# Logit matmuls of the last segment as sixteen 32 by 32 tiles in place of four 32 by 128 tiles

## The chip, the cores and the metric

The kernel runs on one core of one Trainium2 chip. The metric is the time of one execution in device microseconds. A core has a matrix engine (TensorE; PE in the profile, with its weight loads in a row of their own, PEld), VectorE (DVE), ScalarE (ACT), GpSimd (POOL) and a queue for transfers (SP). A matmul multiplies a stationary operand, brought in by a weight load, with a moving operand, of which it takes one column after the other. The array may be used whole or as smaller tiles; the profile writes the rows and columns in use as 128*32 or 32*128.

## The reference

The input is x, 2048 tokens of 512 features, in bfloat16. Two branches are computed from it and mixed by a gate per token.

```python
q, k, v = x @ wq, x @ wk, x @ wv           # 32 heads of 16 features, 4 segments of 512 tokens
for s in range(4):                         # branch a: attention within a segment, and a memory
    logits = einsum('bhqd,bhkd->bhqk', qs, ks) * 16 ** -0.5 + mask
    a_dot = softmax(logits) @ vs
    a_mem = (phi(qs) @ M) / (phi(qs) @ z + 1e-6)
    o[s] = sigmoid(beta) * a_mem + (1 - sigmoid(beta)) * a_dot
    M += phi(ks).T @ vs ; z += phi(ks).sum()
a = o @ wo
b = (gelu(x @ w_gate) * (x @ w_up)) @ w_down        # branch b: 512 -> 1792 -> 512
out = g * a + (1 - g) * b                  # g = sigmoid of a weighted sum of x per token
```

The mask is causal. phi(t) is t + 1 for positive t and exp(t) otherwise.

## The kernel before

All engines follow one written order of tasks (`ORDER`): each word is a task with its engine and its buffers, and the tasks of an engine run in that order. On TensorE the tasks of attention and of the feed-forward branch alternate: groups of q, k, v, gate (`gt`) and up projections (`up`), logit slots (`lg0` to `lg71`), the products with the probabilities (`pv`), memory updates (`M`), memory reads (`den`, `num`), and the down projection with the output projection (`dn`, `wo`). Nearly all of them use four tiles of 128 rows by 32 columns side by side: the helper `mm4` (L385) splits one 128 by 128 matmul into four with 32 output partitions each. The first matmuls of the kernel, up to the first logit slot, use the whole array.

Queries and keys lie transposed in chunks of 128 partitions: 8 heads of 16 features, 512 tokens. A group of 32 partitions holds an even and an odd head. For even heads the stationary operand is 16 rows of `kT`; for odd heads it is 32 rows of `kO`, a copy of the keys with the even head's rows set to zero.

A segment has 18 logit slots, 9 for each pair of chunks. In a slot (`logit_slot`) the loop over `j` goes over the four groups of 32 partitions, thus four heads, and each of the four writes to a PSUM bank of its own (two `lg` tiles of two banks). Only the parts of the triangle that the mask leaves are computed. The slots are of two kinds:

- whole-key slots (`e` is 0 for even heads and 1 for odd heads): 128 keys by 256, 192 or 64 queries. A slot has three parts of these widths in one of two orders, `FULL[0]` (256, 64, 192) or `FULL[1]` (256, 192, 64). That makes 3 x 4 = 12 matmuls with 16 or 32 rows and 128 columns, and 512 moving columns for each `j`. There are 16 of these in a segment.
- merged slots (`e` is 2), two in a segment: 8 parts of 64 queries, 32 matmuls.

After a slot ACT takes the exponential of its two `lg` tiles (L233), POOL sets what the mask forbids to zero (L715, L710), and `pv` uses the result as moving operand (L743). The slots of the last segment are `lg54` to `lg71`, of which `lg56` and `lg65` are merged ones. They begin at 193.3 us and end at 240 us of the span; behind them TensorE has memory reads, products with probabilities and down projections up to 265 us.

The matmuls of a memory update (L858) have 34 moving columns: 8 quads of four column tiles, 32 matmuls in a group.

Of the kernel before, what the change touches and what calls it, by code (L numbers as in the profile page):

```python
# [13 lines left out]
P = 128  # L14
# [5 lines left out]
NSEG = 4  # L20
# [141 lines left out]
class Sched:  # L162
# [10 lines left out]
    def add(self, name, engs, fn, **kw):  # L173
        t = Task(name, [engs] if isinstance(engs, str) else list(engs), fn, **kw)
        self.tasks.append(t)
        return t
# [22 lines left out]
def kernel(  # L199
# [15 lines left out]
    nc = tc.nc  # L215
# [10 lines left out]
    def act(dst, src, func, **kw):  # L226


        k = 1 if func == AF.Gelu_apprx_tanh else 0
        if k != aset[0]:  # L230
            nc.scalar.activation(nil[0][:, 1:2], nil[0][:, 0:1], func)  # L231
            aset[0] = k
        nc.scalar.activation(dst, src, func, **kw)  # L233
# [21 lines left out]
    def lgtile(name="lg"):  # L255
        return plg.tile([P, 2, L], F32, name=name, tag="lg" + S.bank())
# [4 lines left out]
    def rtile(ring, shape, dtype=BF):  # L261
        return rp.tile(shape, dtype, name=ring, tag=ring + S.bank(), bufs=1)
# [398 lines left out]
    def logit_slot(s, t):  # L661
        pr, u = divmod(t, 9)
        gi = s * NSLOT + t
        A = LGT[(s, t)] = {}
        e, w = {0: (0, 0), 1: (0, 1), 3: (1, 0), 4: (1, 1), 5: (0, 0), 6: (0, 1), 7: (1, 0),
                8: (1, 1), 2: (2, 0)}[u]
        cs = [0, 1] if e == 2 else [0 if u < 5 else 1]

        def fn(_):
            TAB["tiled"] = True  # L670
            for h in range(2):
                A[h] = lgtile()
            q, k, o = (QK.get((n, s, pr)) for n in "qko")
            if e == 2:
                parts = [(i, kt, kt * P, HB, (4 * i + kt) * HB) for i in cs for kt in range(KT)]
            else:
                parts = [(cs[0], kt, kt * P + HB + d, n, at) for kt, d, n, at in FULL[w]]
            for i, kt, q0, n, at in parts:
                for j in range(4):
                    a = slice(32 * j, 32 * j + (DH if e == 0 else 32))  # L680
                    l = (k[a, i, kt * P:(kt + 1) * P] if e == 0 else
                         o[a, i, kt, 0:P] if e == 2 else o[a, i, kt, HB:HB + P])
                    nc.tensor.matmul(A[j // 2][:, j % 2, at:at + n], lhsT=l,  # L683
                                     rhs=q[a, i, q0:q0 + n],
                                     start=True, stop=True, tile_position=(32 * j, 0))
        deps = []
        for i in cs:
            c = 2 * pr + i
            deps += [EVQK[(n, s, c)] for n in ("qk", "qo", "qeo")[e]]
        frees = []  # L690
        if gi > 0:
            deps.append(LT[gi - 1])
        if u == 8:
            frees = [(n + "T" if n != "o" else "kO", first_ev[(n, s, pr)]) for n in "qko"]
            if s == 0:
                frees = [((r, pr) if r == "kT" else r, x) for r, x in frees]
        g = add(f"lg{gi}", "PE", fn, cost=240, deps=deps, mode="row",
                alloc=["lg", "lg"], frees=frees)
        LT[gi] = g
        for h in range(2):  # L700
            def fx(_, h=h):
                pT[(s, t, h)] = rtile("pT", [P, 2, L])
                act(pT[(s, t, h)][:, :, :], A[h][:, :, :], AF.Exp, scale=0.25)

            def fa(_, h=h):
                pt = pT[(s, t, h)]
                if e == 2:
                    for z in range(2):
                        v = pt[HB * z:HB * z + HB, :, :].rearrange("p h (g n) -> p (h g) n", n=HB)
                        nc.gpsimd.affine_select(out=v, in_=v, pattern=[[0, 16], [1, HB]],  # L710
                                                compare_op=ALU.is_ge, fill=0.0, base=0,
                                                channel_multiplier=-1)
                    return
                v = pt[:, :, :].rearrange("p h (g n) -> p (h g) n", g=2)[:, :, 0:HB]
                nc.gpsimd.affine_select(out=v, in_=v, pattern=[[0, 4], [1, HB]],  # L715
                                        compare_op=ALU.is_ge, fill=0.0, base=HB,
                                        channel_multiplier=-1)
            x = add(f"ex{gi}{'ab'[h]}", "ACT", fx, kind="exp",
                    deps=[g], alloc=["pT"], frees=[(("lg", h), g)])
            XT_[(gi, h)] = x  # L720
            AT[(gi, h)] = add(f"as{gi}{'ab'[h]}", "POOL", fa,
                              kind="as8" if e == 2 else "as2", deps=[x])
# [371 lines left out]
```

## Time and profile before

| | |
|---|---|
| median of 3 runs | 270.33 us (270.03 to 270.43) |
| the profiled execution | 270.36 us, span 268.6 us |
| granted TensorE clock | 1.000 |
| PE matmuls | 6,276, busy 262.6 us (98% of the span) |
| PE weight loads | 6,276, busy 143.5 us |
| DVE, ACT, POOL busy | 182.7, 222.0, 142.7 us |
| logit matmuls (L683) | 1,024 in 72 slots |
| of these in the slots that the change touches | 192 in 16 slots |

The profile is one execution. A matmul's duration in it runs from its beginning to the modelled end of its results, so matmuls that run side by side or behind each other overlap, and the busy share of PE is not its share of peak. How fast matmuls follow one another is read from their beginnings. Every matmul has its weight load just ahead of it in program order; "pair" below means the two. "Quad" is four matmuls of four tiles that begin within some ns of each other.

### The profile page before, as it was taken

The numbers are of one execution on the slowest core, as the hardware profiler recorded it, in microseconds if no ns is written. First come the engines' busy times: TensorE is split into PE (matmuls) and PEld (weight loads), VectorE is DVE, ScalarE is ACT, GpSimd is POOL, SyncE is SP. The second block draws the span as 40 slices with busy tenths as digits, with TensorE's granted clock in tenths as the row PEclk, the third lists the DMA queues.
The fourth block names the chain that finished last, engine by engine and source line by source line (L and its number), as shares of the span: only waits on it lengthen the run. The fifth ranks groups of instructions, "written<-read, shape, count | busy, mean of one in ns | idle before, by whom it ended". The sixth has DMA issues, their size and how long they took to land.

```text
span 268.6 us, 13714 instructions
## 1 busy us (share of the span) xinstructions
PE 262.6 (98%) x6276; PEld 143.5 (53%) x6276; DVE 182.7 (68%) x367; ACT 222.0 (83%) x260; POOL 142.7 (53%) x262
## 2 busy tenths in 40 slices
PE   8999999999999999989999999999999999999994
PEld 7645455454565545464554546555554555545653
DVE  1552799967776688867876949765785896284712
ACT  2699999999989999999998999987989897882010
POOL 8440665047589166578427275557517287954100
PEclk9999999999999999999999999999999999999999
DMA  6999949322300000200004000200100000100111
GB/s 208 370 242 307 171 45 159 101 83 43 120 2 5 2 2 2 45 2 5 2 4 44 22 2 19 68 5 2 43 5 2 2 2 5 61 4 8 58 51 52
DMA packets 23610, 15.96 MB, mean 59 GB/s; under 512 B 13824, under 2 KB 22528, under 8 KB 23552
## 3 DMA queue, kind: packets, MB, share of 16 engines
q1 hardware_dynamic: 22400, 14.17, 22.7%
q8 instruction: 49, 0.80, 1.3%
q10 hardware_dynamic: 1152, 0.92, 1.0%
q14 instruction: 9, 0.07, 0.1%
HBM read 9.84 MB, written 2.10 MB: 44 GB/s over the span
## 4 chain that ended last, share of the span: by engine, by line
PE 88%; ACT 5%; DVE 4%; issue 1%
PE dn L385 23%; PE up L385 18%; PE gt L385 14%; PE lg L683 8%; PE pv L743 7%; PE v L385 5%; PE q L385 4%; PE k L385 4%; PE k L381 2%; ACT pT L233 2%; ACT L231 1%; ACT G L233 1%; PE num L385 1%; PE warm L381 1%; DVE ebr L622 1%; DVE G L610 1%
## 5 line engine op out<-in xcount | busy, mean ns | idle before, releaser
L233 ACT ACTIVATE pT<-lg 128x1024 bf16<-128x1024 f32 x144 | 137.7, 1029 | 11.1 <-PE lg L683 7.4
L715 POOL TENSOR_SCALAR_AFFINE_SELECT pT<-pT 128x256 bf16<-128x256 bf16 x128 | 52.5, 436 | 61.9 <-ACT pT L233 60.3
L385 PE MATMUL dn<-wdn,G 128*32 128x512 bf16 (+1 forms) x952 | 57.0, 367 | 0.0
L385 PE MATMUL up<-xT,wup 128*32 128x512 bf16 x896 | 56.6, 380 | 0.0
L610 DVE TENSOR_TENSOR G<-up,G 128x512 bf16<-128x512 f32 x56 | 38.5, 687 | 19.8 <-PE up L385 19.0
L385 PE MATMUL gt<-xT,wga 128*32 128x512 bf16 x832 | 48.0, 379 | 0.1
L710 POOL TENSOR_SCALAR_AFFINE_SELECT pT<-pT 64x1024 bf16<-64x1024 bf16 x32 | 37.1, 1160 | 16.5 <-ACT pT L233 11.0
L760 DVE STREAM_TRANSPOSE T<-pv 128x512 f32<-128x512 f32 x32 | 22.7, 711 | 17.8 <-PE pv L743 17.7
L385 PEld LDWEIGHTS <-wga 128*32 128x32 bf16 x832 | 23.4, 97 | 20.7 <-issue 0.4
L385 PEld LDWEIGHTS <-G 128*32 128x32 bf16 x952 | 23.9, 97 | 19.4
L385 PEld LDWEIGHTS <-wup 128*32 128x32 bf16 x896 | 22.9, 96 | 19.4 <-issue 0.2
L233 ACT ACTIVATE G<-gt 128x1024 bf16<-128x1024 f32 x28 | 27.5, 1016 | 3.4 <-PE gt L385 3.3
L231 ACT ACT_TABLE_LOAD x20 | 25.7, 1283 | 0.4
L743 PE MATMUL pv<-pT,vz 128*32 128x256 bf16 (+2 forms) x768 | 22.5, 238 | 0.1
L998 ACT ACTIVATE osb<-dn,omz 128x512 bf16<-128x512 f32 (+1 forms) x6 | 3.7, 616 | 20.8 <-PE dn L385 20.8
L743 PEld LDWEIGHTS <-vz 128*32 128x32 bf16 x768 | 17.2, 97 | 5.8 <-issue 0.6
L385 PEld LDWEIGHTS <-xT 128*32 128x32 bf16 x528 | 13.4, 96 | 12.2 <-DVE xT L786 0.2
L385 PE MATMUL dn<-wo,xT 128*32 128x512 bf16 (+1 forms) x272 | 19.1, 367 | 0.0
L923 POOL TENSOR_SCALAR rm<-Tm 32x32 f32<-32x32 f32 x48 | 15.1, 315 | 7.3 <-DVE Tm L917 4.2
L683 PEld LDWEIGHTS <-kO 32*128 32x128 bf16 x640 | 9.7, 92 | 15.7 <-issue 14.9
L743 PE MATMUL pv<-pT,vh 128*32 128x64 bf16 x512 | 17.6, 193 | 0.0
L683 PE MATMUL lg<-qT,kO 32*128 32x64 bf16 (+2 forms) x640 | 16.9, 217 | 0.5 <-issue 0.5
(107 smaller groups left out, 335.7 us busy)
## 6 DMA issues: line engine op xcount, KB each, us to landing
wup<-in_B_w_up_dram SPq DMA_DIRECT2D x1, 1792.0 KB, 9.4
out_dram<-osb SPq DMA_DIRECT2D x13, 128.0 KB, 1.8
wdn<-in_B_w_down_dram SPq DMA_DIRECT2D x3, 512.0 KB, 4.0
wga<-in_B_w_gate_dram SPq DMA_DIRECT2D x1, 1280.0 KB, 9.5
wdn<-in_A_x_dram SPq DMA_DIRECT2D x2, 512.0 KB, 10.9
wq<-in_A_wq_dram SPq DMA_DIRECT2D x1, 512.0 KB, 4.5
wga<-in_B_w_gate_dram SPq DMA_DIRECT2D x1, 512.0 KB, 5.8
wv<-in_A_wv_dram SPq DMA_DIRECT2D x1, 512.0 KB, 6.7
```

What stands on the lines that cost most here:

```text
L231: nc.scalar.activation(nil[0][:, 1:2], nil[0][:, 0:1], func)
L233: nc.scalar.activation(dst, src, func, **kw)
L381: nc.tensor.matmul(out, lhsT=lhsT, rhs=rhs, start=start, stop=stop)
L385: nc.tensor.matmul(out[a], lhsT=lhsT[:, a], rhs=rhs, start=start, stop=stop, tile_position=(0, 32 * j), skip_group_check=True)
L610: UPT[(s, hs)] = evac("DVE", g, box, lambda e, t: nc.vector.tensor_mul(G[(s, hs // 2)][:, hs % 2, :], t[:, :], G[(s, hs // 2)][:, hs % 2, ...
L683: nc.tensor.matmul(A[j // 2][:, j % 2, at:at + n], lhsT=l, rhs=q[a, i, q0:q0 + n], start=True, stop=True, tile_position=(32 * j, 0))
L710: nc.gpsimd.affine_select(out=v, in_=v, pattern=[[0, 16], [1, HB]], compare_op=ALU.is_ge, fill=0.0, base=0, channel_multiplier=-1)
L715: nc.gpsimd.affine_select(out=v, in_=v, pattern=[[0, 4], [1, HB]], compare_op=ALU.is_ge, fill=0.0, base=HB, channel_multiplier=-1)
L743: nc.tensor.matmul(t[32 * j:32 * j + 32, q0:q0 + n], lhsT=v, rhs=pT[(s, u, j // 2)][:, j % 2, at:at + n], start=(n_ == 0), stop=(n_ == len ...
L760: nc.vector.transpose(TT[key][:, e, :, :].rearrange("p a b -> p (a b)"), t[:, :])
L923: eng_of[e].tensor_scalar_add(RMt[s][32 * j:32 * j + 32, c, :, :], bx["Td"][32 * c:32 * c + 32, :, 2 * j:2 * j + 2], 1e-6)
L998: nc.scalar.activation(bx["o"][:, lo:hi], box["t"][:, 0:hi - lo], AF.Copy, scale=g)
```

## The change

In the last segment's whole-key slots each matmul of 32 (or 16) rows by 128 columns is split into four by columns: the loop over `b` takes 32 keys at a time as stationary operand and writes their 32 output partitions, with the same moving operand. So a part of a slot has 16 matmuls, on tiles of 32 by 32 of the array, in place of 4. All other slots run the loop once, as before.

```diff
-                    nc.tensor.matmul(A[j // 2][:, j % 2, at:at + n], lhsT=l,
-                                     rhs=q[a, i, q0:q0 + n],
-                                     start=True, stop=True, tile_position=(32 * j, 0))
+                    for b in range(4) if s == NSEG - 1 and e < 2 else [None]:
+                        m = slice(0, P) if b is None else slice(32 * b, 32 * b + 32)
+                        nc.tensor.matmul(A[j // 2][m, j % 2, at:at + n], lhsT=l[:, m],
+                                         rhs=q[a, i, q0:q0 + n], start=True, stop=True,
+                                         tile_position=(32 * j, 32 * b if b else 0),
+                                         skip_group_check=b is not None)
```

The matmuls of the 16 slots go from 192 to 768, and the weight loads with them. The tasks, their order and their buffers are the same.

## The prediction

> **What bounds the kernel now.** I read the page's engine table first, then the chain that ended last, cut to the last segment, then the timeline of single slots.
>
> ```profile
> span 268.6 us, 13714 instructions
> PE 262.6 (98%) x6276; PEld 143.5 (53%) x6276; DVE 182.7 (68%) x367; ACT 222.0 (83%) x260; POOL 142.7 (53%) x262
> PE 88%; ACT 5%; DVE 4%; issue 1%
> PE dn L385 23%; PE up L385 18%; PE gt L385 14%; PE lg L683 8%; PE pv L743 7%; PE v L385 5%; PE q L385 4%; PE k L385 4%; PE k L381 2%; ACT pT L233 2%; ACT L231 1%; ACT G L233 1%; PE num L385 1%; PE warm L381 1%; DVE ebr L622 1%; DVE G L610 1%
> ```
>
> TensorE (PE) is busy all the time and carries 88% of the chain. Cut to 190 us and after, the chain is PE without a break up to 265.1 us, where the last evictions and stores follow. The table of waits from 185 us on has no entry for PE, and its weight loads wait for another engine twice, 0.6 us together. So what a logit slot of the last segment costs or saves on PE moves the end one for one: behind the last slot PE still has 25 us of work queued, mostly down projection. Here is that chain around three slots (start, length, what, instructions):
>
> ```profile
> 222.50 0.22 PE up L385 x4
> 222.72 0.33 PE lg L683 x12
> 223.05 0.76 PE dn L385 x12
> 223.81 0.86 PE up L385 x16
> 224.67 0.36 PE lg L683 x32
> 225.03 0.98 PE dn L385 x16
> ```
>
> A slot of 12 matmuls costs 0.33 us, and the merged slot of 32 matmuls of 64 columns (which the edit leaves alone) only 0.36. The timeline of one slot with what stands on both sides of it (PE only; a row's length runs to the end of its last matmul, which includes the pipeline's depth):
>
> ```profile
> 206.07 0.39 PE L385 MATMUL v<-wv,xT 128*32 128x512 bf16 x4
> 206.39 0.40 PE L683 MATMUL lg<-qT,kO 32*128 32x256 bf16 x12
> 206.72 1.05 PE L385 MATMUL up<-xT,wup 128*32 128x512 bf16 x16
> ```
>
> A quad of 512 columns elsewhere begins 0.215 us after the one before (0.86 us for 16 `up` matmuls above), so 0.42 ns per column: 107, 80 and 27 ns for 256, 192 and 64. The slot's first matmul begins 0.31 us after the last `v` quad, not 0.215: about 0.10 us of standstill on the way in. Its last matmul has 64 columns and takes 188 ns by the grouped rows, so it begins 0.40 - 0.19 = 0.21 after the first; with its 27 ns that is 0.24, and the next group begins at 0.33: 0.09 standstill on the way out. In between, 512 columns cost 215 ns plus some 11 ns for the first exposed weight load. In the 16 slots of the segment these lengths repeat to a few ns; slots that end with 192 columns also take 0.33.
>
> **What the change does to this.** In 16 slots (18 of the segment less the two merged ones; 8 run 256, 64, 192 columns, 8 run 256, 192, 64) each of the 3 parts gets 16 pairs of weight load and matmul in place of 4. A slot goes from 12 to 48 pairs, PE from 12,552 instructions to 13,704 (+576 of each kind). Nothing moves: order, banks, waits and the other engines' instructions are as before. The columns streamed per tile stay 512 per slot, so the data time stays 215 ns if 16 tiles run beside each other as 4 do now. Three terms are left.
>
> *Standstill in and out.* Both sides of the slot are 128x32 tiles, the slot becomes 32x32: columns agree, rows still don't. Does the row change alone cost the 0.10? The trace has one such case, the first slot, entered from full 128x128 matmuls (only the rows change):
>
> ```profile
> 14.32 0.38 PE L381 MATMUL q<-xT,wq 128*128 128x512 bf16 x1
> 14.63 0.40 PE L683 MATMUL lg<-qT,kT 16*128 16x256 bf16 x12
> 14.96 0.61 PE L385 MATMUL v<-wv,xT 128*32 128x512 bf16 x7
> ```
>
> Again 0.31 from the last 512 columns to the slot. I take both standstills as unchanged: 0. The way out by a row change alone is not in the trace; bounds 0 and -0.09 us per slot.
>
> *Issue of the pairs.* This is the term that decides. How fast can PE take pairs of load and matmul when the columns are few? The update matmuls `M` (34 columns, 32 pairs, four column tiles) show two paces. One that begins right behind a logit slot:
>
> ```profile
> 175.23 0.38 PE L858 MATMUL M<-vz,pk 128*32 128x34 bf16 x32
> ```
>
> 0.38 less 0.18 for the last matmul: 32 pairs begin in 0.20 us, 6.3 ns each. But behind another `M` group at 44.57 the loads of the gate stream come slower. The weight loads in windows that end at 44.80 and at 44.842:
>
> ```profile
> 44.79 0.09 PEld L385 LDWEIGHTS <-wga 128*32 128x32 bf16 x1
> 44.79 0.13 PEld L385 LDWEIGHTS <-wga 128*32 128x32 bf16 x6
> ```
>
> Five more loads in 0.13 - 0.09 = 0.04 us, with the matmuls between them: the single records stand 8.3 ns apart per pair, 4.1 ns per instruction, and this goes on until 512-column quads let the stream catch up. I read it as a short queue that PE's sequencer fills at 8.3 ns per pair. In the group at 175.23 the sequencer delivers 0.20 / 8.3 = 24 pairs, so about 8 of the 32 lay ready when the standstill ended. For a changed slot: 8 pairs ready, 40 x 8.3 = 332 ns until the last pair begins. The data doesn't hold this up: part two could begin at 120 ns, and its first pair is fed at 75; from its seventh pair on the feed is later than the tile. Then the last tile streams 80 or 27 ns and the 0.09 follows: 0.332 + 0.172 = 0.504 and 0.332 + 0.118 = 0.450, against 0.330. That is +0.174 and +0.120, times 8 each: **+1.39 + 0.96 = +2.35 us**. A matmul behind a just-issued load may add its 8 to 10 ns once (the `up` quad behind a slot is that much late): +0.1 in all. I take +2.4.
>
> Bounds: if the queue were deep enough for the whole slot, the pairs would follow at the 3.6 ns at which the four of a quad begin. Then 256, 64, 192 has its last tile at 120 + 58 + 56 = 234 ns (158 now) and 256, 192, 64 at 120 + 82 + 56 = 258 (212 now): +0.076 and +0.046, **+1.0 us** in 16 slots. If only 8 tiles run at once, each part streams twice: +215 ns and some 60 of skew, 16 x 0.275 = **+4.4 us**. I stay with the feed, the only pace seen past the ready pairs.
>
> *Fetching.* The page has 0.80 MB of instruction packets, 64 bytes for each of PE's 12,552; 1,152 more are 0.07 MB, some 5 packets of 49, and the DMA engines are busy for 0.05 of the stretch from 185 to 242 us: 0. Uncovered, one packet's wait would be a few tenths of a us.
>
> What waits for the slots: the exponentials on ACT start up to 0.17 us later, and so does everything behind them on PE itself, so no new wait; the probabilities are used by PE some slots later.
>
> **Sum.** The profiled execution took 270.36 us (span 268.6 and 1.8 around it), 0.03 above the median of 270.33. 270.36 + 2.4 = 272.8 us, and the difference to the median doesn't matter. A run of this kernel can tell about 0.2%, 0.54 us, from no change.
>
> **Rivals.**
> *The pairs aren't fed, but free* (271.4 us, +1.0, worked out above). For: the queue's depth is inferred from one group; the merged slot begins 32 pairs in 0.23 us with no sign of lack. Against: 32 pairs at 7 ns barely outrun the feed, and 48 do. The Trainium skill, "TensorE: Matmul & The Clock Gate", "Measured speedup vs the span model", counts about 4 ns per further tile and sixteen tiles at 10.6 times one; by that rule alone this rival is the result. The row at 44.79 speaks for a slower pace, and no run here yet shows sixteen tiles. Chance 0.13.
> *Only four tiles of the sixteen run at once.* All traffic of the trace has four in flight: four row tiles or four column tiles. If tiles that share rows queue behind each other, each part streams four times: +3 x 215 = +645 ns a slot, 16 x 0.65 = +10.4, 280.8 us. Against: the four column tiles of `up` share all 128 rows and run side by side. The Trainium skill, same page, "The mechanism", says that a weight load overlaps a running matmul only when its row group differs, which would bring this about; the `up` rows contradict it for the loads of column tiles. Chance 0.09; eight at once (274.8) 0.05.
> *Faster: no standstill.* If the array halts only when the tiles' columns change, 32x32 between 128x32 needs neither the 0.10 nor the 0.09. Per slot 0.147 - 0.188 = -0.04, in sum -0.66: 269.7 us. It decides from 0.15 us saved per slot up. Against it stands the entry at 14.63. Chance 0.05. With the way out alone saved, +0.9: 271.3, inside the range.
> The change does what it says: the listing of after has the 1,152 instructions in these slots and no other.
>
> **How the numbers follow.** Fed pairs 0.68 (272.8, own range 271.9 to 273.6), free pairs 0.13, eight 0.05, four 0.09, no standstill 0.05. The range 271.2 to 275.0 takes in the first three, and leaves out four at once and no standstill. Faster by over 0.2%: 0.03, the larger part of the last case; its rest and small surprises in the cost, 0.03 for the same; slower 0.94.
>
> **What would show it.** After: 16 logit slots of 48 pairs at 0.50 and 0.45 us on the chain in place of 0.33, entry still 0.31 behind the last quad; loads and matmuls 8 ns apart past the first eight pairs; the merged slots still 0.36; all other groups the same. Slots of 0.40 mean a deeper queue, of about 1 us serial tiles, under 0.33 that the standstill has gone.

## The result and the profile after

The changed kernel takes 276.44 us (median of 4 runs, 275.03 to 276.88) against 270.25: ratio 1.022, 95% interval 1.0201 to 1.0240. A second set of five runs, with a second trace, gave 277.19 us, ratio 1.025 (1.0232 to 1.0267). The forecast was 272.8 with a range up to 275.0: the direction was right, and the loss is between two and three times the forecast one.

The profiled execution took 276.88 us. From its page, the lines of the span, of PE, of the instruction packets and of the chain:

```profile
span 275.2 us, 14866 instructions
PE 267.4 (97%) x6852; PEld 149.3 (54%) x6852; DVE 182.2 (66%) x367; ACT 222.7 (81%) x260; POOL 141.1 (51%) x262
q8 instruction: 53, 0.87, 1.3%
PE 80%; SPq 6%; DMA 6%; DVE 4%; ACT 3%; issue 1%; ACTq 0%
```

PE has 576 matmuls and 576 weight loads more, as the diff says, and 53 instruction packets in place of 49. In the segment the chain is still PE's; the transfers in it belong to the start of the kernel. The slot `lg58`, the same one that the prediction showed, with its neighbours (timeline, PE only):

```profile
207.96 0.60 PE L385 MATMUL v<-wv,xT 128*32 128x512 bf16 x8
208.49 0.62 PE L685 MATMUL lg<-qT,kO 32*32 32x256 bf16 x48
209.05 0.40 PE L385 MATMUL up<-xT,wup 128*32 128x512 bf16 x4
```

The next group begins 0.56 us after the slot, not 0.33. The single records of the slot: it begins 309 ns after the last `v` quad (311 before), its last matmul begins 429 ns after its first (213 before), and the `up` quad 125 ns later (117 before). So the way in is what it was, the way out is 8 ns longer, and the inside has doubled. Cut into narrow windows, the timeline shows how. The first row ends its window at 208.665, the second one at 208.78:

```profile
208.49 0.41 PE L685 MATMUL lg<-qT,kO 32*32 32x256 bf16 x32
208.49 0.41 PE L685 MATMUL lg<-qT,kO 32*32 32x256 bf16 x32
```

32 matmuls have begun by 208.665, and none begins in the following 0.115 us. In the single records the first 16 begin within 50 ns, 3.3 ns apart; the second 16 from 119 to 169 ns; then no load and no matmul begins until 304 ns (the 33rd weight load had begun at 143), and from there the pairs follow 8.3 ns apart. The sixteen tiles run beside each other as hoped; the stop in the middle is new.

There is a second new thing. The chain a little later:

```profile
223.04 0.56 PE pv L746 x40
223.59 0.24 PE lg L685 x11
223.84 0.79 issue
224.63 0.36 PE lg L685 x30
```

For 0.79 us PE waits for nothing that the profile shows ("issue"). A like stop lies in a `pv` group at 216.83, 0.61 us long by the single records.

From the beginning of `lg54` to the last matmul the kernel before takes 71.45 us, the changed one 76.79 in this trace and 78.39 in the second. The split slots make up 8 x (0.609 - 0.330) + 8 x (0.555 - 0.330) = 4.0 of the 5.3 and 6.9; the rest, 1.3 and 2.9, is as much as the stops for "issue" amount to beyond the time that would have passed anyway. The first trace had also lost 1.3 us before the segment began (`lg54` at 194.61 against 193.33), where both kernels are the same; in the second trace it begins at 193.36, so that part is the run's.

### The profile page after: what moved, and what is told of

It reads as the page before. It is cut to its first block, busy times and chain, and to the rows that moved or that the text cites. A ratio compares the mean times of both kernels' runs of the same rounds, so it can differ in the third digit from the quotient of the medians.

```text
span 275.2 us, 14866 instructions
## 1 busy us (share of the span) xinstructions
PE 267.4 (97%) x6852; PEld 149.3 (54%) x6852; DVE 182.2 (66%) x367; ACT 222.7 (81%) x260; POOL 141.1 (51%) x262
## 4 chain that ended last, share of the span: by engine, by line
PE 80%; SPq 6%; DMA 6%; DVE 4%; ACT 3%; issue 1%; ACTq 0%
PE dn L385 22%; PE up L385 17%; PE gt L385 12%; PE lg L685 9%; PE pv L746 7%; DMA beta<-in_A_beta_dram 4%; SPq L295 4%; PE v L385 4%; PE q L385 4%; PE k L385 4%; DMA wdn<-in_A_x_dram 2%; ACT pT L233 2%; SPq L323 1%; PE num L385 1%; DVE ebr L622 1%
## 5 line engine op out<-in xcount | busy, mean ns | idle before, releaser
L718 POOL TENSOR_SCALAR_AFFINE_SELECT pT<-pT 128x256 bf16<-128x256 bf16 x128 | 51.0, 423 | 68.7 <-ACT pT L233 67.2
L385 PEld LDWEIGHTS <-wga 128*32 128x32 bf16 x832 | 24.8, 97 | 19.0 <-DMA wga<-in_B_w_gate_dram 0.2
L385 PEld LDWEIGHTS <-xT 128*32 128x32 bf16 x528 | 13.7, 96 | 12.3 <-issue 0.7
L685 PEld LDWEIGHTS <-kO 32*128 32x128 bf16 (+1 forms) x928 | 11.6, 91 | 16.3 <-issue 14.9
L685 PE MATMUL lg<-qT,kO 32*128 32x64 bf16 (+5 forms) x928 | 19.0, 224 | 0.5 <-ACT pT L233 0.4
```

The source lines that it names most:

```text
L385: nc.tensor.matmul(out[a], lhsT=lhsT[:, a], rhs=rhs, start=start, stop=stop, tile_position=(0, 32 * j), skip_group_check=True)
L685: nc.tensor.matmul(A[j // 2][m, j % 2, at:at + n], lhsT=l[:, m], rhs=q[a, i, q0:q0 + n], start=True, stop=True, tile_position=(32 * j, 32 ...
```

## The experiments

Three theories. **1**: PE holds at most 64 instructions (32 pairs) that have not finished; the 33rd pair gets in when the first matmul ends. (Here every matmul has one load, so no run can tell a limit of 64 instructions from one of 32 matmuls.) **2**: every pair costs a fixed 9 ns. **3**: instructions come to PE in blocks of 256, and a block takes a certain time to fetch, whatever PE does.

**The changed kernel again**, no edit.

> The changed kernel once more, for a second trace. Of its 6.6 us in the first trace, 4.0 lie in the sixteen slots (0.61 and 0.56 us in place of 0.33), 1.4 in two stalls at instruction numbers 10429 and 10941 of TensorE, and 1.3 had come before the segment began. Theory 1 (64 instructions in flight): the slots show 0.61 and 0.56 again, to a few ns. Theory 3 (blocks of 256 instructions that have to be fetched): the two stalls are at the same instruction numbers again, 189 above a multiple of 256, and of like size. Rival: stalls that come from another engine move or vanish. The 1.3 us ahead of the segment, where the two programs are the same, should change from run to run: lg54 begins anywhere from 193.3 to 194.7 us. Median 276.4.

Measured: 277.19 us. The twelve slots in which no stop for instructions falls again take 0.608 to 0.610 and 0.555 to 0.557 us; pair 33 begins at 305 to 307 ns. The stops of over 0.3 us, in numbers counted over PE's loads and matmuls: 10429 (0.65 us) and 10941 (0.70) again, and new ones at 9661, 10685 and 12476 (0.37, 0.56, 0.91). All stand at 188 or 189 above a multiple of 256. The tasks there are of several kinds (`pv`, `up`, `lg`). What didn't hold is "of like size": the stops vary from run to run. The 1.3 us ahead of the segment was absent here.

**64 columns first.**

```diff
                 parts = [(cs[0], kt, kt * P + HB + d, n, at) for kt, d, n, at in FULL[w]]
+                if s == NSEG - 1:
+                    parts = [parts[(1, 2)[w]], parts[0], parts[(2, 1)[w]]]
```

> The changed kernel with the 64-column part issued first in all sixteen slots (64, 256, 192). Theory 1 (TensorE holds 64 instructions that are not finished; pair 33 gets in when the first matmul ends, then pairs follow at the sequencer's 8.3 ns): the first matmul now takes 0.188 us in place of 0.278, so pair 33 begins at 0.21 in place of 0.30 us, the last one at 0.34, and with 0.18 behind it a slot is 0.52 us against 0.61 and 0.56 (mean 0.58): -0.065 us times 16 = -1.0, median 275.4. Theory 2 (every pair costs its 9.1 ns, 430 / 47, wherever it stands): the last pair begins at 0.43 as before, all slots end with 192 columns and take 0.61: +0.4 us, 276.8. The theory of the prediction (8 pairs ready, 8.3 ns for each further one): the last pair at 0.33 whatever the order, no gain against the other order.

Measured: 276.96 us (ratio 1.0245, 1.0225 to 1.0265). The slot at 207.96, its row and the group behind it (timeline):

```profile
207.96 0.60 PE L687 MATMUL lg<-qT,kO 32*32 32x64 bf16 x48
208.49 0.40 PE L385 MATMUL up<-xT,wup 128*32 128x512 bf16 x4
```

0.529 us a slot, pair 33 at 225 ns, the last at 350. The first matmul takes 198 ns, not the 188 that I expected, and 198 + 26 = 224. That is theory 1 and neither of the others: the order alone moves pair 33 by 80 ns, as the end of the first matmul moves. But the time didn't fall by the 0.85 us that the slots lost. From `lg54` to the last matmul it is 78.19 us: 3.2 us of longer slots and 3.5 of stops, at 9661, 10429, 10685, 10941, 11708 and 12476. What the slots gave, the stops took in this trace.

**The eight-slot kernel, in both orders.** These two show the same without stops. The first splits the even heads' slots only:

```diff
-                    for b in range(4) if s == NSEG - 1 and e < 2 else [None]:
+                    for b in range(4) if s == NSEG - 1 and e == 0 else [None]:
```

> Sixteen tiles in the eight slots of the even heads alone, four tiles in those of the odd heads. Theory 1: 4 x 0.28 + 4 x 0.225 = +2.0 us in the slots. Theory 3: the blocks of 256 instructions take longer than in the changed kernel, so most of the 1.4 us of stalls goes: 272.3 to 272.9 in all. If the whole loss of 6.2 us goes with the number of split slots: +3.1, 273.4.

Measured: 272.58 us (ratio 1.0086, 1.0067 to 1.0105). Split and unsplit slots side by side in the chain:

```profile
215.12 0.56 PE lg L685 x48
215.68 0.67 PE pv L746 x40
216.35 0.86 PE k L385 x16
```

From `lg54` to the last matmul 73.42 us, +1.97, and the eight slots account for 2.02. No stop in the segment. Half the split slots cost little more than a third of the loss, since these eight bring no stop. The second kernel adds the order above for these eight slots:

> Sixteen tiles in the eight slots of the even heads alone, and these with the 64-column part first. With all sixteen slots split, this order made the slots shorter (0.53 for 0.61 and 0.56 us) but the time stayed, and stalls for instructions grew by as much. If fetching was what took the gain, it must show here, where the eight-slot kernel has no stall in the segment: 4 x 0.079 + 4 x 0.026 = -0.4 us from lg54 to the last matmul (73.4 to 73.0), median 272.2. If the order gives the gain back in another way (the exponentials, the 192 columns at the end), it stays at 73.4.

Measured: 272.00 us (ratio 1.0077, 1.0048 to 1.0106); the two medians differ by less than their intervals. The trace does tell: the eight slots take 0.528 to 0.530 us, and `lg54` to the last matmul 73.04, 0.38 less than the 73.42. Without stops the order's gain arrives whole.

**Eight tiles of 32 by 64.**

```diff
-                    for b in range(4) if s == NSEG - 1 and e < 2 else [None]:
-                        m = slice(0, P) if b is None else slice(32 * b, 32 * b + 32)
+                    for b in range(2) if s == NSEG - 1 and e < 2 else [None]:
+                        m = slice(0, P) if b is None else slice(64 * b, 64 * b + 64)
...
-                                         tile_position=(32 * j, 32 * b if b else 0),
+                                         tile_position=(32 * j, 64 * b if b else 0),
```

> Eight tiles of 32 by 64 in place of sixteen of 32 by 32: 24 pairs a slot, 48 instructions. Theory 1: fewer than 64 in flight, so no halt; the last tile begins some 13 to 27 ns later than now, slots of 0.34 to 0.36 us, 16 x 0.02 = +0.3: 270.6 us. Theory 2 (9.1 ns a pair): 23 x 9.1 = 0.21 us, hidden behind the 256, 192, 64 order, +0.05 in the other: +0.5, 270.8. If tiles narrower than the array's columns cost something by themselves (a slow weight load, rows shared by tiles), a good part of the +6 us remains: above 272. Theory 3: 192 more pairs move the block borders; no stall over 0.3 us in the last segment is expected, since a block still takes over 3.5 us there.

Measured: 270.77 us (ratio 1.0021, 1.0006 to 1.0036). The slot `lg58`:

```profile
208.19 0.43 PE L685 MATMUL lg<-qT,kO 32*64 32x256 bf16 x24
208.55 0.40 PE L385 MATMUL up<-xT,wup 128*32 128x512 bf16 x4
```

Slots of 0.356 to 0.360 us, no stop in the middle, and in the segment none for instructions. So tiles that share their rows cost little by themselves: with 24 pairs a slot loses 0.03 us. I take that for the skew of eight tiles in place of four; no run tests it alone.

**The merged slots with 64 pairs.** The kernel before, with this split where `e` is 2, in the two merged slots of the last segment.

```diff
-                    for b in range(2) if s == NSEG - 1 and e < 2 else [None]:
+                    for b in range(2) if s == NSEG - 1 and e == 2 else [None]:
```

> The kernel before, with the two merged slots of the last segment on eight tiles of 32 by 64: 64 pairs of 64 columns in place of 32, no other slot changed. Theory 1 (64 instructions, 32 pairs, in flight): the first matmul takes 0.198 us, so pair 33 begins at 0.198 + 0.026 = 0.22 us and the last at 0.22 + 31 x 0.0083 = 0.48, against 0.225 now: +0.25 us for each of the two slots, 270.8. Theory 2 (9.1 ns a pair): 63 x 9.1 = 0.58, and pair 33 at 0.29. The prediction's theory (8 ready, then 8.3 ns): 0.46, and pair 33 at 0.21 with the pairs at an even pace from the ninth on.

Measured: 270.46 us (ratio 1.0016, 0.9998 to 1.0034). The slot `lg65`, in the kernel before (first row) and here with the group behind it:

```profile
224.61 0.42 PE L683 MATMUL lg<-qT,kO 32*128 32x64 bf16 x32
224.59 0.71 PE L685 MATMUL lg<-qT,kO 32*64 32x64 bf16 x64
225.23 0.40 PE L385 MATMUL dn<-wdn,G 128*32 128x512 bf16 x4
```

Single records: 32 matmuls begin within 139 ns, then there is a stop to 238 or 239, and 31 more follow at 8.3 to 8.4 ns to 497. The first matmul here takes 212 ns, and 212 + 26 = 238. This settles theory 1 against 2 (pair 33 at 290, the last at 580) and against the prediction's reading (an even pace from the ninth pair on). It also shows the rule with other tiles, other columns and no sixteen-tile slot in the kernel. And it rules out a limit of two unfinished matmuls per tile: pair 33 is the third use of its tile in a sixteen-tile slot, but the fifth here. The rule holds beyond the slots: in none of the thirteen traces does a matmul begin earlier than 26 ns after the end of the matmul 32 places ahead of it.

**Moving the block borders.** Four kernels test theory 3: 32 or 192 instructions more in the warm-up, in the changed kernel and in the one before.

```diff
-NWARM = 22
+NWARM = 20
+NTINY = 18
...
             for i in range(NWARM):
                 mm4(t[:, 0, 0:P], warm, warm, True, True)
+            for i in range(NTINY):
+                c = 32 * (i % 4)
+                nc.tensor.matmul(t[c:c + 32, 1, 0:24], lhsT=warm[:, c:c + 32], rhs=warm[:, 0:24],
+                                 start=True, stop=True, tile_position=(0, c),
+                                 skip_group_check=True)
```

For 192 these are 14 and 104.

> The changed kernel with 32 TensorE instructions more in the warm-up (20 warm-up matmuls of 128 columns and 18 of 32 by 24 in place of 22), so that every later instruction stands 32 numbers further on in its block of 256. Theory 3 (a block of 256 instructions can't be had in less than about 3.4 us): summing what each block lacks of 3.4 us, in the trace with the stalls taken out, gives 2.7 us as it is and 1.9 us with this shift: 276.2 us. The stalls stand again at 189 above a multiple of 256, thus at other tasks than before. Rival (stalls are waits of these tasks for another engine): the same tasks stall, 277 us.

> The same 32 instructions more in the warm-up of the kernel before. Theory 3: its blocks lack 0.3 us of 3.4 in all, the stall at number 5310 (0.5 to 0.7 us) above all, and nothing with this shift: -0.3 to -0.6, 269.6 to 269.9 us. Rival: no change but for the warm-up, 270.2 to 270.4.

> The changed kernel with 192 instructions more in the warm-up (14 full and 104 small matmuls). Theory 3: with this shift the blocks lack 5.8 us, 3.1 more than now: 280 us, with stalls of up to 1.2 us in the last segment and one of 1.3 us near 5117. Rival: 277 us, and the warm-up's own 0.1 or 0.2.

> The same 192 instructions more for the kernel before. Theory 3: its blocks lack 1.3 us, 1.0 more than now, in the stretch near 117 us alone: 271.2. So the change costs 4.0 + 4.5 = 8.5 us at this shift, and 4.0 + 1.9 = 5.9 at a shift of 32. Rival: the change costs the same 6 to 7 us at any shift.

| kernel | median | ratio, interval | stops over 0.3 us in the last segment, in the kernel's own numbers |
|---|---|---|---|
| changed, +32 | 276.40 | 1.0211 (1.0168 to 1.0254) | 10685, 10941, 11197, 11452, 12476 |
| before, +32 | 270.21 | 1.0006 (0.9986 to 1.0026) | none |
| changed, +192 | 277.36 | 1.0259 (1.0224 to 1.0293) | 10685, 11197, 12732 |
| before, +192 | 271.37 | 1.0036 (1.0010 to 1.0062) | none |

The places came out as theory 3 has them: 188 or 189 above a multiple of 256 in each kernel's own numbering, so at other instructions of the work. Some fall in another task; with 32 more, those at 10941 and 12476 stay in their slots (`lg63` and `lg71`), 32 instructions earlier. With 32 more, a stop also stands in an `up` group that runs freely without them; this is its chain:

```profile
218.36 0.61 PE lg L691 x41
218.97 0.75 PE up L386 x10
219.72 0.56 issue
220.29 0.81 PE up L386 x9
```

The sizes did not: +3.1 us was expected with 192, and 277.36 is what the changed kernel took in its second set (277.19) within the intervals. The stop of 1.3 us expected near 5117 didn't come; one of 0.50 us stood at 5310. A block that took 2.46 us there brought no stop. So "no block in under 3.4 us" is too strict a law; a part of the next block must already lie ready. The two kernels before don't decide: with 32 the stop near 118 us that theory 3 removes is gone from the trace (0.68 us at 5310 in the first trace), but it is also missing in both traces of the changed kernel, where that stretch is the same, and the time is the same; with 192 the time rose by what was expected, but the stop at 5310 is no longer than without (0.63).

**The edit in the second segment.**

```diff
-                    for b in range(4) if s == NSEG - 1 and e < 2 else [None]:
+                    for b in range(4) if s == 1 and e < 2 else [None]:
```

> The same edit in the second segment (lg18 to lg35, 89 to 133 us) in place of the last one. Theory 1: slots of 0.61 and 0.56 again, +4.0 us less what slots lose that wait for their PSUM buffer inside (two of them, 0.2 us each). Theory 3: blocks of 256 instructions take 3.8 to 6.5 us there in the kernel before, except one of 3.2 near 118 us, so with the added instructions stalls come only in the few tight ones: 0.3 to 0.8 us, fewer than the 1.3 to 2.9 of the last segment. 274.3 to 275.0 in all. If the stalls belong to the edit and not to the density, 276.5 to 277.

Measured: 277.00 us (ratio 1.0255, 1.0221 to 1.0290). The slots are 0.555 to 0.557 and 0.607 to 0.611 us wherever nothing else stops them, but my forecast of few stops was wrong. The chain at the largest:

```profile
118.00 0.31 PE M L861 x32
118.31 1.14 PE pv L746 x63
119.45 1.69 issue
121.14 0.20 PE pv L746
```

It is at number 5821 (189 above a multiple of 256, 1.88 us by the single records), with two more at 6333 and 7101 (0.34 and 0.86). I had taken the block times from the kernel before; with 576 pairs more several of the blocks fall to 2.5 to 3.8 us. By the time alone, the other case of the expectation (stops that belong to the edit, 276.5 to 277) fits as well. Against it stand the places, 189 above a multiple of 256, and stops at such places (189 or 190) where nothing was edited: at 5310 in the kernel before, at 7869 (0.49 us) in the trace with 64 columns first, at 1726 (0.49 us) in that of the eight tiles of 32 by 64. So the stops come with the density of instructions and not with the last segment, and at these densities both segments pay.

**The fetch itself**, from the single records of packets on the instruction queue in these traces. They are 16,384 bytes long, 64 for each of 256 instructions. In no trace does a packet begin less than 3.37 us after the one before it. For the stop at 223.65 a packet runs from 222.00 to 223.20, and PE goes on at 224.63, 1.43 us after its end; at 216.83 it is 1.45; in the second segment's long stop 1.35. In all the stops of over 0.32 us at these places, 32 in the thirteen traces, it is 1.27 to 1.58. Where PE has stood, the next packet mostly begins about 1.1 us after PE goes on. A packet takes some 1.0 us. Adding up gives an estimate of 1.1 + 1.0 + 1.4 = 3.5 us for 256 instructions: one block at a time, 13.7 ns an instruction, 27 ns a pair. The 512-column quads use up a pair in 54 ns and a split slot one in 12.

## Why the prediction was wrong, point by point

- *What bounds the kernel* held: PE carries the segment, and what the slots lose arrives in the time. In the eight-slot kernel it did to within 0.05 us.
- *Standstill in and out*: taken as unchanged, measured 0.309 for 0.311 us in, and 0.007 to 0.008 more on the way out, which was the forecast exposed load. The rival without standstill has fallen: rows that differ are enough, and entering 32 by 32 tiles from 128 by 32 costs the same 0.10 us as entering 32 by 128.
- *Issue of the pairs* failed, and it is the term that decides. I read the pace behind the `M` groups as a short queue of 8 pairs that is filled at 8.3 ns a pair. The 8.3 ns were right, the queue wasn't. PE takes 32 pairs at 3 to 7 ns, then nothing until the oldest matmul ends (277 + 26 ns), and only then the 8.3 ns set in: 0.304 + 15 x 0.0083 = 0.43 us to the last pair, where I had 0.33. Mean +0.252 a slot in place of +0.147, 4.0 us in place of 2.35. The rows of before held this: in the `M` group at 44.57 the slow pace sets in with the 30th matmul, at 44.771. The matmul 32 places ahead of it, one of the `k` quad in front of the group, begins at 44.366 and lasts 379 ns, and 44.366 + 0.379 + 0.026 = 44.771. I looked at the pace and not at what set it off. That 8 pairs "lay ready" came from the group at 175.23, where 32 pairs begin without a stop; it has no 33rd pair of its own that could have told the two readings apart.
- *Fetching* was put at 0, on the ground that the DMA engines are idle. This term failed too, and it weighs as much: the issue term came out 1.65 us too small, and the stops cost 1.3 and 2.9 us in the two traces. Bytes were the wrong measure; what counts is the time of one fetch. The "few tenths of a us" for one uncovered packet came from no row; the stops of over 0.3 us in these two traces lasted 0.37 to 0.98 us. The stop in the kernel before at 119.4 (0.68 us by the single records), in a dense stretch, was there to be seen, in its chain:

```profile
119.32 0.28 PE lg L683 x23
119.60 0.49 issue
120.09 0.26 PE lg L683 x9
```

- *The rivals*: free pairs (1.0 us) were the case for two parts of a slot, until the 32 pairs are used up; within a burst the pairs begin 3.3 ns apart. The Trainium skill, "TensorE: Matmul & The Clock Gate", "Measured speedup vs the span model", has about 4 ns for a further tile, and the trace agrees for these bursts. The Trainium skill, same page, states a queue depth of 64 for TensorE in the table at its head; the stop at 32 pairs agrees. Four tiles at once has fallen: sixteen run side by side. The Trainium skill, same page, "The mechanism", lets a weight load overlap a running matmul only when its row group differs; the trace shows otherwise for tiles of the same rows, since 16 loads and matmuls begin alternately within 50 ns.
- *No new waits from other engines*: held. The upper end of the range, 275.0, stood on eight tiles at once (274.8), which isn't what happened.

What stays open is how long a given stop for instructions gets: the same kernel had stops of 0.98 and 0.70 us at the same number, and the law of 3.4 us a block forecast neither the sizes nor which blocks stop; only the place within a block was right.

## What to carry to other kernels

Count pairs of weight load and matmul, not only columns. A run of more than 32 pairs, of which 32 begin before the first matmul has finished, stops until it has. A stretch that needs less than about 3.5 us (the estimate above) for 256 instructions can outrun its own instruction stream. The finer split here left the columns per tile as they were, so it paid both and gained nothing. When "issue" stands in the chain, number the instructions: in these traces the stops at a fixed place in blocks of 256 came with the fetches, and shifting the program moved them to other instructions.

## What the runs showed of the hardware that was not expected

- At most 32 pairs (64 instructions) are unfinished on PE at a time, by the ends that the profile models: pair 33 begins some 26 ns after the end of the first matmul (at 225 ns behind one of 198, at 238 behind 212, at 304 to 306 behind 278).
- Behind such a stop pairs follow 8.3 ns apart; before it, sixteen tiles of 32 by 32 begin 3.3 ns apart.
- Instructions arrive in packets of 256, which begin at least 3.37 us apart, and after a stop PE goes on some 1.4 us (1.27 to 1.58) after the packet's end.
